# A retention and mixture-of-experts kernel on one core: the first chunk in four transfers with its values on GpSimd and six filling products, one expert choice behind the masks, one eviction ahead of three transposes, and the last block scaled by ScalarE alone

## The chip, the cores and the metric

The kernel runs on one core of a Trainium2 chip. The metric is the device time of one execution in microseconds (us); several executions are timed and their median is taken. In the profile, PE is TensorE (matrix products), PEld its loading of stationary operands, DVE is VectorE, ACT is ScalarE, POOL is GpSimd and SP is SyncE, which here issues nearly all loads. A letter q behind an engine's name (SPq) marks its instruction queue, where transfers are issued.

## The reference, cut to what matters

```python
# q, k, v: (4, 8, 768, 64) float32, that is batches, heads, tokens, width of a head
state = zeros(B, H, D, D)
for t in range(S):
    state = gamma[h] * state + outer(k[:, :, t], v[:, :, t])
    y[:, :, t] = scale * (q[:, :, t] @ state)
x = y.transpose(0, 2, 1, 3).reshape(3072, 512)

logits = x @ w_gate                            # 8 experts
expert_idx = argmax(logits, axis=1)
gate_w = softmax(logits)[expert_idx]
for e in range(8):
    xe = x[expert_idx == e]
    out[expert_idx == e] = gate_w * (relu(xe @ w1[e]) @ w2[e])   # 512 -> 1024 -> 512
```

## The kernel before

**Two stages.** The first is the retention (until some 105 us of the profile's clock), the second the experts (until 392 us). The 3072 tokens are cut into 24 chunks `g` of 128 tokens, six to a batch (`CPB`); `c = g % CPB` is the place in the batch. The retention is computed chunk by chunk in closed form: scores of a chunk against itself under a causal mask, plus the carried state.

**A chunk's steps.** `load(g)` brings the chunk's 1 MB in four parts of 512 columns: q turned, k turned, v natural, k natural (256 KB each). `scale(g)` multiplies v by the decay constants (`vs`), on GpSimd or VectorE. `scores(g)` makes 8 products of q and k into two PSUM tiles `sp` (one for each of the two heads of a pair), and VectorE multiplies each by the mask into `Sb`. `update(g)` adds the chunk to the state `U`, and ScalarE copies it to `ub`. `carry(g)` multiplies q by the state of the chunk before, into `Y`; `output(g)` adds the scores times the values to `Y`, and VectorE evicts `Y`, scaled, into `xT`. `rows(g)` turns `xT` back to token rows (`tr`, copied by ScalarE to `xrow`), and `logits` makes the gate's logits of two chunks (`lp`, `lg`).

**Gating.** The chunks' tokens are gated in six groups (`GROUPS`, first chunk and count). For each group, "choose" finds the largest logit on VectorE (`mx`, `ed`, `EA`, the one-hot choice), "soft" prepares the softmax with ScalarE, "rank" counts the tokens of each expert ahead of each token with the product `pf` on PE (`EA` against a triangle `us`), "slots" makes of it a row number (`KEY`), "weights" the softmax weight (`GW`), "label" writes both into the row. Then GpSimd scatters the rows, sorted by expert, to memory (`x_sorted`). Group 2 holds chunks 12 to 15; its choice stands at the end of chunk 16.

**Experts.** Each expert's tokens are fetched sorted, turned by VectorE (`turn_slices`, STREAM_TRANSPOSE), and split in a high part (ScalarE) and a low part (VectorE or GpSimd), as the weights are; each product of float32 precision is three products of high and low parts (`ph` into the hidden layer, `py` out of it). Before the retention has ended, the first 320 rows of expert 0 are fetched and turned (`turn_early`, in chunk 22), and pieces of their products (`fill`) stand between the last gating steps. `py` blocks of 128 rows are scaled by the gate weight into `yo` (`put_rows`), and GpSimd scatters them to the output. The last block of the last expert has 104 rows.

**What sets the order.** The program is under `tc.manual_schedule()`: each engine works off its instructions in the order in which the code is written, and semaphores order the engines against each other. SP's transfers take eight counters in turn, so its ninth waits for the first to have landed. Chunks 0 to 3 are loaded in halves of two parts each; the first is issued ahead of everything else. The constants `cs` and the small operand `gs` of the decay table are issued by ScalarE's queue. While PE has no data, it runs `WARM = 10` filling products into `warm` (128x512, bf16), and later one product makes the decay table (`decay`, copied to `buf`, where `G` lies). The score buffers `sp` are two, so the scores of the next chunk wait for the masks of this one.

## Time and profile before

| | |
|---|---|
| runs, median (lowest to highest) | 399.66 us (399.08 to 399.91), 3 runs |
| profiled execution: its time, its span | 400.06 us, 398.3 us |
| mean granted clock of PE in the profiled execution | 0.995 |
| PE busy | 390.3 us, 98% of the span, 3236 instructions |
| PEld busy | 356.5 us, 89% |
| DVE busy | 240.3 us, 60% |
| POOL busy | 185.2 us, 46% |
| ACT busy | 142.4 us, 36% |
| bytes moved | 81.53 MB, mean 205 GB/s |

The span is the time between the first and the last instruction of the profile; the execution's own time holds 1.76 us more. The rows by line that are shown below begin with the start and the busy time of a group (in us), then engine, line, operation, output and inputs with their tile shapes, and the number of instructions; in square brackets stands how long the engine was idle just before, and what ended that. The line numbers are those of the kernel before.

### The profile page before, as it was taken

To read this page: it belongs to the slowest core of one execution; us is meant where nothing else is said; L and a number is where in the kernel's file an instruction comes from. 1 tells how busy PE (TensorE), PEld (TensorE's weight loads), DVE (VectorE), ACT (ScalarE), POOL (GpSimd) and SP (SyncE) were. 2 spreads that over 40 slices of the span, in tenths; PEclk is the share of its full clock that TensorE was granted. 3 is DMA by queue.
4 is the path that set the end of the run, shared out by engine and by line. 5 is a ranking of instruction groups with operands and counts; after the bars stand their busy time and mean duration, and the time that the engine had idled before them with its cause. 6 is when DMAs were issued, how large, how long until landed. Compare 5 with 4: busy or idle time off the path is not lost. (4 is left out here: it accounts for less than half of the span.)

```text
span 398.3 us, 8240 instructions
## 1 busy us (share of the span) xinstructions
PE 390.3 (98%) x3236; PEld 356.5 (89%) x3236; DVE 240.3 (60%) x468; ACT 142.4 (36%) x249; POOL 185.2 (46%) x176
## 2 busy tenths in 40 slices
PE   8999999999999999999999999999999999999994
PEld 4888878787899889999999999999999999999972
DVE  3555757685744578573866477477737657665310
ACT  2224435224411455531542344054334416423100
POOL 1647959655260517200584077028406813740741
PEclk9999999999999999999999999999999999999998
DMA  8999999975058839547452755465564647430111
GB/s 273 422 419 420 418 416 420 324 297 149 2 216 174 327 117 305 214 167 162 166 182 92 190 183 213 84 209 165 177 152 157 234 83 232 146 133 0 54 47 48
DMA packets 42316, 81.53 MB, mean 205 GB/s; under 512 B 4444, under 2 KB 18144, under 8 KB 39844
## 3 DMA queue, kind: packets, MB, share of 16 engines
q1 hardware_dynamic: 36768, 67.46, 51.2%
q0 software_dynamic: 5360, 13.49, 9.1%
q8 instruction: 26, 0.43, 0.4%
q14 instruction: 14, 0.11, 0.1%
q10 hardware_dynamic: 148, 0.04, 0.1%
HBM read 65.90 MB, written 15.68 MB: 205 GB/s over the span
## 5 line engine op out<-in xcount | busy, mean ns | idle before, releaser
L738 POOL DMA_INDIRECT out<-Z,sidx x90 | 104.9, 1165 | 138.8 <-DVE Z L894 113.5
L133 DVE TENSOR_TENSOR wlo<-raw,whi 128x1024 fp32r<-128x1024 f32 x54 | 65.5, 1215 | 14.1 <-ACT whi L132 13.8
L132 ACT CAST whi<-raw 128x1024 fp32r<-128x1024 f32 (+1 forms) x72 | 67.3, 950 | 7.3 <-DMA raw<-w 7.3
L1034 PE MATMUL py<-hl,whi 128*128 128x452 f32 (+5 forms) x192 | 67.0, 349 | 0.0
L1034 PE MATMUL py<-hh,wlo 128*128 128x452 f32 (+5 forms) x192 | 66.8, 348 | 0.0
L1034 PE MATMUL py<-hh,whi 128*128 128x452 f32 (+5 forms) x192 | 66.8, 348 | 0.0
L1014 ACT ACTIVATE hh<-ph 128x452 fp32r<-128x452 f32 (+6 forms) x56 | 28.3, 507 | 81.5 <-PE ph L1009 81.5
L1009 PE MATMUL ph<-xh,wlo 128*128 128x452 f32 (+6 forms) x224 | 50.1, 345 | 0.0
L1009 PE MATMUL ph<-xh,whi 128*128 128x452 f32 (+6 forms) x224 | 50.1, 345 | 0.0
L1009 PE MATMUL ph<-xl,whi 128*128 128x452 f32 (+6 forms) x224 | 50.0, 345 | 0.0
L1015 DVE SCALAR_TENSOR_TENSOR hl<-ph,hh 128x452 fp32r<-128x452 f32 (+6 forms) x56 | 32.0, 574 | 29.7 <-ACT hh L1014 29.2
L1009 PEld LDWEIGHTS ph<-xh,whi 128*128 128x128 f32 x224 | 40.8, 188 | 0.8
L1009 PEld LDWEIGHTS ph<-xh,wlo 128*128 128x128 f32 x224 | 40.8, 188 | 0.8
L1009 PEld LDWEIGHTS ph<-xl,whi 128*128 128x128 f32 x224 | 40.7, 188 | 0.7
L1034 PEld LDWEIGHTS py<-hh,wlo 128*128 128x128 f32 x192 | 36.0, 188 | 0.8
L1034 PEld LDWEIGHTS py<-hl,whi 128*128 128x128 f32 x192 | 36.0, 188 | 0.7
L1034 PEld LDWEIGHTS py<-hh,whi 128*128 128x128 f32 x192 | 36.0, 188 | 0.7
L251 DVE TENSOR_TENSOR Sb<-sp,cs 128x512 f32<-128x512 f32 x48 | 30.8, 684 | 7.4 <-PE sp L248 7.4
L760 ACT CAST xh<-buf 128x512 fp32r<-128x512 f32 (+7 forms) x26 | 14.3, 556 | 56.5 <-DVE buf L753 56.5
L133 POOL TENSOR_TENSOR wlo<-raw,whi 128x512 fp32r<-128x512 f32 (+1 forms) x18 | 24.9, 1403 | 12.7 <-ACT whi L132 10.5
L738 POOL DMA_INDIRECT x_sorted<-xrow,KEY x24 | 24.2, 1010 | 13.1 <-issue 6.5
L889 DVE STREAM_TRANSPOSE Z<-py 128x416 f32<-128x416 f32 (+3 forms) x24 | 15.0, 626 | 24.4 <-PE py L1034 24.4
(163 smaller groups left out, 535.3 us busy)
## 6 DMA issues: line engine op xcount, KB each, us to landing
raw<-w SPq DMA_DIRECT2D x32, 1024.0 KB, 5.6
qkv_w<-qkv SPq DMA_DIRECT2D x12, 1024.0 KB, 18.3
qkv_t<-qkv SPq DMA_DIRECT2D x7, 1024.0 KB, 17.8
qkv_t<-qkv SPq DMA_DIRECT2D x8, 512.0 KB, 6.8
buf<-x_sorted SPq DMA_DIRECT2D x12, 211.2 KB, 4.8
x_sorted<-cs SPq DMA_DIRECT2D x6, 260.0 KB, 5.6
buf<-x_sorted SPq DMA_DIRECT2D x8, 195.0 KB, 4.7
out<-Z,sidx POOLq DMA_INDIRECT x90
```

The costliest lines, as they stand in the source:

```text
L132: nc.scalar.copy(out=hi[:, h], in_=raw[:, h])
L133: engine.tensor_tensor(out=lo[:, h], in0=raw[:, h], in1=hi[:, h].bitcast(F32), op=ALU.subtract)
L251: nc.vector.tensor_tensor(out=Sb[:, r], in0=sps[r], in1=causal.unsqueeze(1).broadcast_to([P, NP, C]), op=ALU.mult)
L738: sc = tc.nc.gpsimd.indirect_dma_start(out=dst, out_offset=bass.IndirectOffsetOnAxis(ap=index, axis=0), in_=rows, in_offset=None, bounds_c ...
L760: nc.scalar.copy(out=xh[:, :, c0:c0 + w], in_=xt[:, :, t0:t0 + w])
L889: nc.vector.transpose(out=Zs[e][:, 0:nb, k, :], in_=py[:, 0:32 * nb].rearrange("p (j c) -> p j c", c=32))
L1009: nc.tensor.matmul(out=ph[:, :cap], lhsT=wparts[e, f // 4][a][:, kd, fo:fo + P], rhs=x[:, kd, :cap], start=(n == 0), stop=(n == 3 * KD - 1))
L1014: nc.scalar.activation(out=hh[:, :cap], in_=ph[:, :cap], func=AF.Relu)
L1015: nc.vector.scalar_tensor_tensor(out=hl[:, :cap], in0=ph[:, :cap], scalar=0.0, in1=hh[:, :cap].bitcast(F32), op0=ALU.max, op1=ALU.subtract)
L1034: nc.tensor.matmul(out=py[:, :cap], lhsT=a[:, f % 4, k * P:(k + 1) * P], rhs=x[:, :cap], **se)
```

## The change

Five places are edited.

1. **The start.** Chunk 0 comes in four transfers of 256 KB and chunk 1 in a half and two quarters. The host lays q and k out anew, so that the first quarter holds q and k of the head pairs 0 and 1, and the second those of the pairs 2 and 3; `turned(g, i, r, p)` finds them. ScalarE's queue issues the constants `cs` ahead of `gs`. The values of chunk 0 are scaled by GpSimd. Six filling products instead of ten.
2. **Chunk 1.** The carry products stand ahead of the update.
3. **The third choice.** "choose" and "soft" of group 2 stand in chunk 17 (`FULL - 1`), behind the masks of chunk 18, instead of at the end of chunk 16, and its weights behind its slots.
4. **The early turns.** All three pieces of `turn_early` stand behind `output(22)`; before, the first stood ahead of it.
5. **The last block.** One ScalarE instruction of 512 columns scales it; before, VectorE scaled the first half and ScalarE the second.

```diff
-WARM = 10
+WARM = 6
...
-        def turned(g, i):
-            return qs[g][:, i].rearrange("a (p t) -> a p t", p=NP)
+        def turned(g, i, r, p):
+            at = i * 2 * C + p % 2 * C
+            return qs[g][half[r], p // 2, at:at + C]
...
-        def turn_early(i):
+        def turn_early():
...
-            part = pieces[1:] if i else pieces[:1]
-            for j, w, _ in part:
+            for j, w, _ in pieces:
                 turn_slices(nc, xt0, first["xg"], j, w)
...
-        load(0, halves[0])
+        quarters = [slice(i, i + 1) for i in range(4)]
+        load(0, quarters[0])
         gs = buf[0:2, 4 * NP * C:4 * NP * C + P + NP * C]
+        nc.scalar.dma_start(out=cs[:, 0:NFIRST], in_=cst[:, 0:NFIRST])
         nc.scalar.dma_start(out=gs, in_=gdec)
-        nc.scalar.dma_start(out=cs[:, 0:NFIRST], in_=cst[:, 0:NFIRST])
-        load(0, halves[1])
-        for part in halves:
+        for part in quarters[1:]:
+            load(0, part)
+        for part in (halves[0], *quarters[2:]):
             load(1, part)
...
-        scale(0, nc.vector)
+        scale(0)
...
+        def choose_group(i):
+            stages[i] = gating(i)
+            stages[i]["choose"]()
+            stages[i]["soft"]()
...
             if 1 < g < last:
                 scores(g + 1)
-            if g in ranked:
+            if g == FULL - 1:
+                choose_group(2)
+            elif g in ranked:
                 stages[ranked[g]]["weights"]()
...
-            if g == 1:
-                update(g)
             if g < last:
                 carry(g)
             if g == 1:
+                update(g)
                 scores(g + 1)
...
-            if g == last - 1:
-                turn_early(0)
             output(g)
...
             if g == last - 1:
-                turn_early(1)
+                turn_early()
...
                 if g != FULL + 1:
                     s["slots"]()
+                if g == FULL - 1:
+                    s["weights"]()
                 s["advance"]()
...
-        parts = (slice(0, 2), slice(2, 4)) if e == E1 and j == len(widths[e]) - 1 else (slice(0, 4),)
-        for i, k in enumerate(parts):
-            args = dict(out=sliced(yo[:w, :])[:, k], in_=featured(py[:w, :])[:, k])
-            if i:
-                nc.scalar.activation(func=AF.Copy, scale=meta[:w, j, 1:2], **args)
-            else:
-                nc.vector.tensor_scalar(in0=args["in_"], out=args["out"], scalar1=meta[:w, j, 1:2], scalar2=None,
-                                        op0=ALU.mult)
+        args = dict(out=sliced(yo[:w, :]), in_=featured(py[:w, :]))
+        if e == E1 and j == len(widths[e]) - 1:
+            nc.scalar.activation(func=AF.Copy, scale=meta[:w, j, 1:2], **args)
+        else:
+            nc.vector.tensor_scalar(in0=args["in_"], out=args["out"], scalar1=meta[:w, j, 1:2], scalar2=None, op0=ALU.mult)
```

PE at the start of the program, before: the last filling product, the scores of chunk 0 (one wait for the first half's counter), the decay table, the update (it waits for `vs` from DVE), and the output products.

```order
L489 MATMUL warm<-ones 128x512
L248 MATMUL sp<-qkv_t 128x128 [waits DMAHW1_49]
L248 MATMUL sp<-qkv_t 128x128 x7
L510 MATMUL decay<-buf 128x512 [waits DMAHW0_49]
L263 MATMUL U<-vs,qkv_t 64x64 [waits DMAHW3_49,DVE_49]
L263 MATMUL U<-vs,qkv_t 64x64 x7
L287 MATMUL Y<-Sb,vs 64x128 [waits DVE_49]
```

The same place on PE, of the changed kernel:

```order
L487 MATMUL warm<-ones 128x512
L249 MATMUL sp<-qkv_t 128x128 [waits DMAHW1_49]
L249 MATMUL sp<-qkv_t 128x128 x3
L249 MATMUL sp<-qkv_t 128x128 [waits DMAHW3_49]
L249 MATMUL sp<-qkv_t 128x128 x3
L508 MATMUL decay<-buf 128x512 [waits DMAHW2_49]
L264 MATMUL U<-vs,qkv_t 64x64 [waits DMAHW5_49,Pool_49]
L264 MATMUL U<-vs,qkv_t 64x64 x7
L287 MATMUL Y<-Sb,vs 64x128 [waits DVE_49]
```

The score products now wait for two counters, one for each quarter, and the update waits for the values from GpSimd (Pool) instead of VectorE.

DVE in chunks 16 and 17, before: `lg` closes the logits, the rows from `mx` to `sh` are the third choice, the two rows `Sb` are the masks of chunk 18, `GW` the weights, and `rk` takes up the ranking product `pf`.

```order
L348 TENSOR_REDUCE lg_1168<-lp 128x16 [waits PE_49]
L371 TENSOR_REDUCE mx_1243<-lg_1168 128x4 [waits DVE_49]
L372 TENSOR_REDUCE lp<-lg_1168 128x32 [waits Activation_49]
L373 TENSOR_TENSOR lp<-lp,mx_1243 128x32 [waits DVE_49]
L374 TENSOR_TENSOR lp<-lp,cs 128x32 [waits DVE_49]
L377 TENSOR_REDUCE ed_1244<-lp 128x4 [waits DVE_49]
L378 TENSOR_TENSOR EA<-lp,ed_1244 128x32 [waits DVE_49]
L380 TENSOR_TENSOR sh_1251<-lp,mx_1243 128x32
L251 TENSOR_TENSOR Sb<-sp,cs 128x512 [waits PE_49] x2
L413 TENSOR_REDUCE GW<-exs 128x4 [waits Activation_49]
```

The same place on DVE, of the changed kernel:

```order
L348 TENSOR_REDUCE lg_1167<-lp 128x16 [waits PE_49]
L252 TENSOR_TENSOR Sb<-sp,cs 128x512 [waits DVE_49,PE_49]
L252 TENSOR_TENSOR Sb<-sp,cs 128x512 [waits PE_49]
L371 TENSOR_REDUCE mx_1257<-lg_1167 128x4 [waits DVE_49]
L372 TENSOR_REDUCE lp<-lg_1167 128x32 [waits Activation_49]
L373 TENSOR_TENSOR lp<-lp,mx_1257 128x32 [waits DVE_49]
L374 TENSOR_TENSOR lp<-lp,cs 128x32 [waits DVE_49]
L377 TENSOR_REDUCE ed_1258<-lp 128x4 [waits DVE_49]
L378 TENSOR_TENSOR EA<-lp,ed_1258 128x32 [waits DVE_49]
L380 TENSOR_TENSOR sh_1265<-lp,mx_1257 128x32
```

The masks have moved ahead of the seven instructions of the choice; the weights (`GW`) now stand further down, behind `KEY`.

DVE in chunk 22, before: `xt` are the three transposes of the early rows (the first waits for their fetch), `xT` is the eviction of the chunk's output.

```order
L348 TENSOR_REDUCE lg_1625<-lp 128x16 [waits PE_49]
L753 STREAM_TRANSPOSE xt_1649<-xg_1542 128x4x4x32 [waits DMAHW6_49,DMAHW5_49,DMAHW7_49,DMAHW0_49,Pool_49]
L293 TENSOR_TENSOR xT<-Y,buf 128x4x128 [waits PE_49]
L753 STREAM_TRANSPOSE xt_1649<-xg_1542 128x4x4x32
L753 STREAM_TRANSPOSE xt_1649<-xg_1542 128x2x4x32
```

The same place on DVE, of the changed kernel:

```order
L348 TENSOR_REDUCE lg_1624<-lp 128x16 [waits PE_49]
L293 TENSOR_TENSOR xT<-Y,buf 128x4x128 [waits PE_49,Pool_49]
L757 STREAM_TRANSPOSE xt_1658<-xg_1541 128x4x4x32 [waits DMAHW2_49,DMAHW1_49,DMAHW3_49,DMAHW0_49,Pool_49]
L757 STREAM_TRANSPOSE xt_1658<-xg_1541 128x4x4x32
L757 STREAM_TRANSPOSE xt_1658<-xg_1541 128x2x4x32
```

The eviction has changed places with the first transpose.

More of the change, by code (lines that the diff above doesn't have):

```diff
@@ L243, in scores @@
             Sb = wk.tile([P, 2, NP, C], F32, name="Sb")
-            q, kt = turned(g, 0), turned(g, 1)
             sps = [ps_s.tile([P, NP, C], F32, name="sp") for _ in range(2)]
@@ L247, in scores @@
                 for r in range(2):
-                    nc.tensor.matmul(out=sps[r][:, p, :], lhsT=kt[half[r], p, :], rhs=q[half[r], p, :],
+                    nc.tensor.matmul(out=sps[r][:, p, :], lhsT=turned(g, 1, r, p), rhs=turned(g, 0, r, p),
                                      start=True, stop=True)
@@ L271, in carry @@
             if c > 0:
-                q = turned(g, 0)
                 for m in range(2):
@@ L277, in carry @@
                             nc.tensor.matmul(out=Y[half[o], r, m * C:(m + 1) * C], lhsT=ubs[(g - 1) % 3][half[r], p, :],
-                                             rhs=q[half[r], p, :], start=(m == 0), stop=False, skip_group_check=True)
+                                             rhs=turned(g, 0, r, p), start=(m == 0), stop=False, skip_group_check=True)
         def output(g):
@@ L437, in fetch_early @@
             fetch_rows(xg0, 0, NJ0)
-        def turn_early(i):
+        def turn_early():
             pieces = [(a // 32, min(P, EARLY - a), eng)
                       for a, eng in zip(range(0, EARLY, P), (nc.gpsimd, nc.vector, nc.vector))]
-            if i == 0:
-                first["xt"] = rawp.tile([P, KD, EARLY], F32, name="xt0", tag="raw")
-                first["x"] = [wp.tile([P, KD, EARLY], F32R, name=n, tag="w", bufs=11) for n in ("xh0", "xl0")]
-                early.extend(early_pieces(tc, wk, wp, ps_m, ps_s, ps_1, wparts, first["x"], first))
-            xt0, x = first["xt"], first["x"]
-            part = pieces[1:] if i else pieces[:1]
-            for j, w, _ in part:
+            xt0 = rawp.tile([P, KD, EARLY], F32, name="xt0", tag="raw")
+            first["x"] = x = [wp.tile([P, KD, EARLY], F32R, name=n, tag="w", bufs=11) for n in ("xh0", "xl0")]
+            early.extend(early_pieces(tc, wk, wp, ps_m, ps_s, ps_1, wparts, x, first))
+            for j, w, _ in pieces:
                 turn_slices(nc, xt0, first["xg"], j, w)
-            for j, w, _ in part:
+            for j, w, _ in pieces:
                 cut_high(nc, x[0], xt0, j, w)
-            for j, w, eng in part:
+            for j, w, eng in pieces:
                 cut_low(nc, eng, *x, xt0, j, w)
@@ L593, in retention_moe @@
                 nc.scalar.copy(out=wgs[:, :, 0:E], in_=k_("gates").rearrange("p (k e) -> p k e", k=NP))
-            if g in chosen or g == last:
-                i = chosen.get(g, 4)
-                s = stages[i] = gating(i)
-                s["choose"]()
-                s["soft"]()
+            if g in chosen and g != FULL - 2:
+                choose_group(chosen[g])
+            if g == last:
+                choose_group(4)
             if g == last:
@@ L1161 @@
     arrays = {
-        "qkv": np.stack([transposed(q), transposed(k), natural(v), natural(k)], axis=3).reshape(NCH, P, 4, DM),
+        "qkv": np.concatenate([np.stack([transposed(a).reshape(NCH, P, 2, 2 * C) for a in (q, k)], axis=3)
+                               .reshape(NCH, P, 2, DM), natural(v).reshape(NCH, P, 1, DM),
+                               natural(k).reshape(NCH, P, 1, DM)], axis=2),
         "w1": reordered(moe_w1, 1), "w2": np.ascontiguousarray(moe_w2), "cst": cst, "gdec": gdec,
```

## The prediction

> **What bounds the kernel now.** I read the page first, then the cores, then the order in time at each place that the change touches.
>
> ```profile
> span 398.3 us, 8240 instructions
> core 0: 398.3 us, clock 0.995
> ```
>
> PE carries the program nearly from end to end, so the question at each place is which wait of PE the edit shortens, and whether PE then meets another one. The mean clock says how long PE ran at half rate: 0.005 of 398.3 us is 1.99 us lost, that is 3.98 us at half. The first product starts at 1.08 (below), so full rate came at about 5.06.
>
> The start, in order of time (start, duration, engine, line, operation; in brackets what ended the idle time before it):
>
> ```profile
> 1.08 4.35 PE L489 MATMUL warm<-ones 128*128 128x512 bf16 x10 [1.08 <-DVE ones L155]
> 5.36 1.16 PE L248 MATMUL sp<-qkv_t 64*128 64x128 f32 x16
> 6.45 1.12 PE L510 MATMUL decay<-buf 2*128 2x512 f32 x2
> 6.64 0.69 DVE L235 TENSOR_TENSOR vs<-qkv_t,cs 128x512 f32<-128x512 f32 x1 [4.94 <-DMA cs<-cst]
> 7.25 1.28 DVE L251 TENSOR_TENSOR Sb<-sp,cs 128x512 f32<-128x512 f32 x2
> 7.50 0.69 PE L263 MATMUL U<-vs,qkv_t 128*64 128x64 f32 x16
> 7.61 0.59 ACT L511 COPY buf<-decay 128x512 f32<-128x512 f32 x1 [4.40 <-PE decay L510]
> 8.23 0.37 ACT L266 COPY ub<-U 128x256 f32<-128x256 f32 x1
> 8.59 0.88 PE L287 MATMUL Y<-Sb,vs 128*64 128x128 f32 x12 [0.16 <-DVE Sb L251]
> 9.08 1.04 POOL L235 TENSOR_TENSOR vs<-qkv_t,cs 128x512 f32<-128x512 f32 x1 [7.98 <-DMA qkv_t<-qkv]
> 9.39 1.16 PE L248 MATMUL sp<-qkv_t 64*128 64x128 f32 x16
> 10.58 1.29 DVE L251 TENSOR_TENSOR Sb<-sp,cs 128x512 f32<-128x512 f32 x2 [0.31 <-PE sp L248]
> 11.70 1.39 PE L248 MATMUL sp<-qkv_t 64*128 64x128 f32 x16
> 13.48 0.38 SPq L124 DMA_DIRECT2D raw<-w  x1
> 14.63 1.16 PE L248 MATMUL sp<-qkv_t 64*128 64x128 f32 x16
> ```
>
> PE runs ten filling products until 5.36, one every 0.43 us, and chunk 0's score products follow at once. U then waits for the scaled values (vs), which DVE makes only at 6.64, because the constants cs come late. DVE does the masks (Sb) after that, so the output products pause until 8.59.
>
> When a transfer lands is read from SP. Each transfer takes one of eight counters in turn, and SP's ninth waits until the first has landed, so the row that takes up a counter again marks a landing:
>
> ```profile
> 4.82 0.34 SPq L222 DMA_DIRECT2D qkv_t<-qkv  x1
> 10.97 0.33 SPq L222 DMA_DIRECT2D qkv_w<-qkv  x1
> ```
>
> The first is chunk 0's first half (512 KB); the second is chunk 2's first half. The row at 13.48 above marks chunk 3's first half in the same way. The rates of the transfers, stretch by stretch (last column GB/s; the fourth row is a stretch of weight loads with rows of 2 KB, as the quarters have):
>
> ```profile
> 2.00:3.00 1.00, 1.00 (x4) 0.36 (x3) 0.00 (x0) 1.00 (x1) 0.00 (x0) 1.00 0.79 217
> 3.00:4.00 1.00, 1.00 (x3) 0.30 (x2) 0.00 (x0) 0.19 (x1) 0.00 (x0) 1.00 0.95 250
> 10.00:20.00 10.00, 10.00 (x170) 8.06 (x168) 5.87 (x10) 2.41 (x6) 6.66 (x8) 1.00 1.03 422
> 172.00:173.70 1.70, 1.70 (x10) 1.56 (x9) 1.16 (x2) 0.81 (x1) 0.00 (x0) 1.00 1.05 411
> ```
>
> **The start: quarters, constants first, vs on GpSimd, six products.** Six products end at 1.08 + 6 x 0.43 = 3.64. The first quarter is half of what landed at 4.82. At 217 to 250 GB/s, 256 KB less take 1.0 to 1.2 us less, so it lands at 3.6 to 3.8. It may land as late as 4.8, where the half landed (the last rival), and not much before 3.0, since 217 GB/s move only 217 KB in the row from 2.00 to 3.00; I take 3.7. PE answers about 0.15 later, at 3.85. Half of the score products (0.42 at full rate, so 0.85 at half) end at 4.7. The second quarter lands like the old half, at 4.8, and the other half runs from 4.95 to 5.4. The decay product follows and takes 1.05 (6.45 to 7.50), to 6.45. The values are the third quarter: 256 KB at 422 are 0.62 us, so 5.4 to 5.5. The constants start ahead of the second quarter and should be in by then. GpSimd pays 1.04 (row 9.08) where DVE paid 0.69, so vs stands at 6.65, and U starts 0.17 later (7.33 to 7.50 before) at 6.8, against 7.50. That the gate for U moves to POOL delays nothing there: POOL's next work, the values of chunk 1, came in at 9.08 and comes about 0.6 earlier as a quarter. The fourth quarter lands at 6.1 to 6.4, before U needs it.
>
> DVE is free for the masks at 5.6 and done by 6.9, so the pause ahead of 8.59 goes. U and the output products are 0.51 + 0.98, which brings chunk 1's scores to 8.3 instead of 9.39. They, the carry product and U of chunk 1 (the swap of these two costs nothing: both stand between the same neighbours, 9.39 + 1.09 to 11.70) take 2.31 us and end at 10.6.
>
> There PE meets the next wait: chunk 2 lands at 10.97. Its bytes are the same, and SP's three more issues are hidden, because the transfers already queued last past 8 us. But 1.5 MB now come in rows of 2 KB, at 411 instead of 422 at worst, 0.1 us more. So chunk 2's scores start at 11.1 to 11.25 against 11.70. They took 1.39 there and 1.16 elsewhere, because the masks of chunk 1 freed the score buffers late (10.58 + 1.29); these masks are early now, and 0.23 goes too. Gain 0.45 to 0.6 and 0.23: I take **0.75**. Chunk 3 landed at 13.48 for products at 14.63, so it allows 1.0, and from there nothing on PE waits for a load. A bound from above is 1.09 (what chunk 1's scores gain), from below 0 while the clock opens as before.
>
> **The third choice behind the masks (g = 17).**
>
> ```profile
> 75.48 1.16 PE L248 MATMUL sp<-qkv_t 64*128 64x128 f32 x16
> 76.09 0.19 DVE L371 TENSOR_REDUCE mx<-lg 128x4 f32<-128x32 f32 x1
> 77.10 0.19 DVE L378 TENSOR_TENSOR EA<-lp,ed 128x32 bf16<-128x32 f32 x1
> 77.17 0.43 PE L287 MATMUL Y<-Sb,vs 128*64 128x128 f32 x2
> 77.30 1.28 DVE L251 TENSOR_TENSOR Sb<-sp,cs 128x512 f32<-128x512 f32 x2
> 78.18 1.03 PE L287 MATMUL Y<-Sb,vs 128*64 128x128 f32 x14 [0.57 <-issue]
> 79.14 0.19 PE L387 MATMUL pf<-EA,us 128*128 128x32 bf16 x1
> ```
>
> The choice (mx to EA, 1.20 us) moves from the gap in which DVE waits for the scores to behind the masks. Masks start 1.19 after their scores (9.39 to 10.58), so at 76.67, and end at 77.9; EA then ends at 79.1, and the ranking products (pf) can start at 79.15. They start at 79.14 now, because PE lost about 0.8 us between 77.17 and 78.18, waiting for nothing that the profile shows. So PE has to wait for EA exactly as long as that pause lasted: **0**, whether the pause comes again or not, within 0.1. The masks that come 0.6 earlier help nobody, since the scores that need their buffers stand behind pf. On DVE the values and the eviction behind the choice are 0.6 later, and the weights move behind the keys, with ACT's label behind them: 1.2 us on ACT, which PE meets again only at its logits, and it is idle enough there. At worst 0.3.
>
> **The eviction ahead of the early turns (g = 22).**
>
> ```profile
> 98.94 1.05 PE L287 MATMUL Y<-Sb,vs 128*64 128x128 f32 x16
> 99.59 0.71 DVE L753 STREAM_TRANSPOSE xt<-xg 128x512 f32<-128x512 f32 x1 [1.61 <-DMA xg<-x_sorted]
> 100.23 0.65 DVE L293 TENSOR_TENSOR xT<-Y,buf 128x512 f32<-128x512 f32 x1
> 101.03 0.67 PE L277 MATMUL Y<-qkv_t,ub 64*64 64x128 f32 x16 [0.23 <-ACT xh L760]
> 101.53 0.93 ACT L760 CAST xh<-xt 128x512 fp32r<-128x512 f32 x2 [0.57 <-DVE xt L753]
> 103.06 0.54 PE L793 MATMUL ph<-xh,whi 128*128 128x320 f32 x2
> ```
>
> PE waits for xT (100.88 + 0.15). Y ends at 99.95, so without the transpose xT runs from 100.05 to 100.7 and PE starts at 100.87: **0.16** gained. The three transposes then follow from 100.6, the last cast of xh ends at about 102.8 (102.46 before), and the early products want it at 102.9. That cover is 0.1 thin; past it the gain shrinks to 0. Between 0 and 0.25.
>
> **The last block by ScalarE alone.**
>
> ```profile
> 391.99 0.39 PE L1032 MATMUL py<-whi,hl 128*104 128x512 f32 x1
> 392.42 0.48 DVE L881 TENSOR_SCALAR yo<-py,meta 104x256 f32<-104x256 f32 x1 [4.81 <-PE py L1032]
> 392.94 0.47 ACT L879 ACTIVATE yo<-py,meta 104x256 f32<-104x256 f32 x1 [16.74 <-DVE yo L881]
> 393.72 1.01 POOL L738 DMA_INDIRECT out<-yo,sidx  x1 [4.86 <-ACTq L725]
> ```
>
> The two halves run one after the other: ACT waited for DVE. One ACT instruction of 512 columns costs 0.47 and the 256 columns more, priced by 0.59 - 0.37 = 0.22 (rows 7.61 and 8.23): 0.69, from 392.42 to 393.11 instead of 393.41. All behind it follows: **0.30**. Between 0.2 (as if the longer row cost half as much again) and 0.4.
>
> **Sum.** 0.75 + 0 + 0.16 + 0.30 = 1.2 us. The profiled execution took 400.06 (the span and 1.76 around it), 0.40 above the median of 399.66. Its sum is 398.85; against the median the same gain gives 398.5. A measurement tells 0.2%, 0.8 us, from no change.
>
> **Rivals.**
> A later clock: PE has a gap at 3.64 and a broken stream until 5. If that starts the count again, full rate comes 3.98 after 3.85, at 7.8. The scores then end at 5.7, decay at 7.6, U at 8.25, output at 9.25, and chunk 2's scores start at 11.55 and end 0.35 earlier instead of 0.75: 398.9. Against it: the gap is 0.2 us in 4, and at 77.17 PE paused 0.8 without leaving full rate (the mean clock has no room for it). [...]
>
> The pause at 77.17 is an accident of the profiled run (its time lies above all three others). Where the usual run has no pause, PE would be 0.75 earlier there (masks end at 78.58, the next scores start then instead of at 79.35), and the moved choice takes just that away: 399.2.
>
> Slower: the clock opens two stretches late, at 3.85 + 2 x 3.98 = 11.8, if products that fill half the rows and wait for quarters do not count as work. PE is then at half rate for all of chunks 0 and 1; every microsecond past 7.8 costs 0.5, and chunk 2's scores end 1.6 later than before: 400.8. It decides from an opening at about 9.5 on.
>
> The quarters land no earlier than the half: then the scores run from 4.95 to 6.0, U starts at 7.1, and chunk 2's landing still decides. The time stays.
>
> **Chances.** As forecast 0.52 (its own range 398.0 to 398.8), a later clock 0.20, no pause in the usual run 0.20, slower 0.08. Of the forecast about 0.44 lie beyond 0.2%, of the two middle ones together another 0.10: faster 0.54, same 0.37, slower 0.09. The range goes from 397.6 (the upper bounds 1.09 + 0.25 + 0.4 give 397.9, less 0.3 for a median of three runs, since the three shown lie 0.8 apart) to 399.8, which leaves out the slow case.
>
> **What the next profile would show.** The first scores at about 3.85 in two pieces; U near 6.8, released by POOL; no pause in the first output products; chunk 2's scores at 11.1 to 11.25, released by the DMA; pf released by DVE's EA about 1.0 behind the output products; the carry of chunk 23 about 1.95 behind the output of chunk 22; one ACT row of 104x512 near 0.69 and the scatter 0.3 behind it; a mean clock of 0.995. A clock of 0.990 or less, or scores of twice their length after 5.1, make it wrong.

## The result, and the profile after

The changed kernel takes 401.61 us in the median of 15 runs (400.41 to 403.56), against 399.66 (15 runs, 399.01 to 400.43) before: a ratio of 1.0054, with a 95% interval of 1.0035 to 1.0074. It is slower, where 1.2 us of gain were forecast. Its runs fall apart: seven lie at 400.41 to 400.81, two at 401.61 and 402.36, six at 403.10 to 403.56. Even the lowest is above the median of before. The profiled execution took 403.19, 3.13 above that of before (400.06), so it belongs to the upper group.

The head of its page and the row of its core:

```profile
span 401.4 us, 8237 instructions
core 0: 401.4 us, clock 0.996
```

The start on PE, GpSimd and VectorE, in the timeline (columns as before):

```profile
1.08 2.74 PE L487 MATMUL warm<-ones 128*128 128x512 bf16 x6 [1.08 <-DVE ones L155]
4.17 2.28 PE L249 MATMUL sp<-qkv_t 64*128 64x128 f32 x16 [0.34 <-DMA qkv_t<-qkv]
5.97 1.04 POOL L237 TENSOR_TENSOR vs<-qkv_t,cs 128x512 f32<-128x512 f32 x1 [4.88 <-DMA qkv_t<-qkv]
6.37 2.07 PE L508 MATMUL decay<-buf 2*128 2x512 f32 x2
8.37 1.12 PE L264 MATMUL U<-vs,qkv_t 128*64 128x64 f32 x16
9.28 1.92 PE L287 MATMUL Y<-Sb,vs 128*64 128x128 f32 x16
11.13 1.90 PE L249 MATMUL sp<-qkv_t 64*128 64x128 f32 x16
12.96 0.67 PE L277 MATMUL Y<-qkv_t,ub 64*64 64x128 f32 x16
14.18 1.39 PE L249 MATMUL sp<-qkv_t 64*128 64x128 f32 x16
```

The data come 0.3 to 0.4 later than forecast (first scores at 4.17 against 3.85, values done at 7.01 against 6.65). But every product up to 12.9 takes nearly twice as long as in the profile of before: the decay product 2.07 instead of 1.12, the output products 1.92 instead of 1.09 without a wait, chunk 1's scores 1.90 instead of 1.16. Full rate opens at 12.7. (The trace keeps a record of the granted clock, from which the profile's clock figures are averaged. Its first entry, full rate, is at 12.72 us. The profile counts the time ahead of the first entry as 1.00, though the products there take twice their time.) Chunk 2's scores start at 14.18 instead of 11.70: **2.48 lost**.

Chunk 17:

```profile
79.06 0.67 PE L277 MATMUL Y<-qkv_t,ub 64*64 64x128 f32 x16
79.66 1.09 PE L287 MATMUL Y<-Sb,vs 128*64 128x128 f32 x16
81.37 0.19 DVE L378 TENSOR_TENSOR EA<-lp,ed 128x32 bf16<-128x32 f32 x1
81.71 0.19 PE L387 MATMUL pf<-EA,us 128*128 128x32 bf16 x1 [0.96 <-DVE sh L380]
```

PE now waits 0.96 for the choice, where it paused before. From the carry to the ranking products there are 2.65 us against 2.57: 0.09 lost.

Chunks 22 and 23, first of before, then of the changed kernel:

```profile
101.03 1.28 POOL L767 TENSOR_TENSOR xl<-xt,xh 128x512 fp32r<-128x512 f32 x1 [2.90 <-ACT xh L760]
102.18 1.03 DVE L767 TENSOR_TENSOR xl<-xt,xh 128x512 fp32r<-128x512 f32 x2 [0.36 <-ACT xh L760]
103.26 0.68 DVE L293 TENSOR_TENSOR xT<-Y,buf 128x512 f32<-128x512 f32 x1
104.86 0.19 DVE L378 TENSOR_TENSOR EA<-lp,ed 128x32 bf16<-128x32 f32 x1
105.79 0.19 PE L387 MATMUL pf<-EA,us 128*128 128x32 bf16 x1
109.93 0.75 PE L793 MATMUL ph<-xh,whi 128*128 128x320 f32 x4
```

```profile
103.28 1.62 DVE L757 STREAM_TRANSPOSE xt<-xg 128x512 f32<-128x512 f32 x3
103.52 0.67 PE L277 MATMUL Y<-qkv_t,ub 64*64 64x128 f32 x16
104.72 1.27 POOL L771 TENSOR_TENSOR xl<-xt,xh 128x512 fp32r<-128x512 f32 x1 [4.01 <-ACT xh L764]
105.26 1.61 DVE L771 TENSOR_TENSOR xl<-xt,xh 128x512 fp32r<-128x512 f32 x2 [0.36 <-ACT xh L764]
106.93 0.68 DVE L293 TENSOR_TENSOR xT<-Y,buf 128x512 f32<-128x512 f32 x1
108.53 0.19 DVE L378 TENSOR_TENSOR EA<-lp,ed 128x32 bf16<-128x32 f32 x1
108.87 0.18 PE L387 MATMUL pf<-EA,us 128*128 128x32 bf16 x1
111.93 0.19 PEld L816 LDWEIGHTS acc<-hh,whi 128*128 128x128 f32 x1 [0.36 <-ACT xrow L305]
113.35 0.75 PE L797 MATMUL ph<-xh,whi 128*128 128x320 f32 x4
```

The carry of chunk 23 starts at 103.52 against 101.03, so the edit gained 0.08 there (2.57 late before it, 2.49 after). Then VectorE falls behind: its two low parts take 1.61 instead of 1.03, the eviction of chunk 23 comes 3.67 later than before, the choice EA 3.67, the ranking products 3.08, and the second batch of early products 3.42. PE has **lost 0.93** between 103.5 and 113.4. In the profile of before, GpSimd's low part was nearly done (102.31) when VectorE began its own; now the two run side by side.

The end:

```profile
395.41 0.39 PE L1032 MATMUL py<-whi,hl 128*104 128x512 f32 x1
395.84 0.69 ACT L880 ACTIVATE yo<-py,meta 104x512 f32<-104x512 f32 x1 [16.22 <-PE py L1032]
396.83 1.01 POOL L742 DMA_INDIRECT out<-yo,sidx  x1 [4.55 <-ACTq L729]
```

The last product is 3.42 later, the scatter 3.11: 0.31 gained. The sum is 2.48 + 0.09 - 0.08 + 0.93 - 0.31 = 3.11, and the measured difference of the two profiled executions 3.13: the rows account for it. This is the sum for one execution of the upper group, not for the median.

### The profile page after: what moved, and what is told of

Its sections match the earlier page's. It is cut to its first block, busy times and chain, and to the rows that moved or that the text cites. A ratio compares the mean times of both kernels' runs of the same rounds, so it can differ in the third digit from the quotient of the medians.

```text
span 401.4 us, 8237 instructions
## 1 busy us (share of the span) xinstructions
PE 393.0 (98%) x3232; PEld 358.8 (89%) x3232; DVE 240.7 (60%) x466; ACT 141.9 (35%) x249; POOL 185.8 (46%) x177
## 4 chain that ended last, share of the span: by engine, by line
issue 39%; PE 35%; POOL 16%; DMA 5%; DVE 2%; ACT 1%; POOLq 1%; DVEq 0%; ACTq 0%
POOL out L742 16%; PE sp L249 7%; PE Y L287 5%; DMA out<-Z,sidx 4%; PE acc L816 3%; PE U L264 3%; PE Y L277 3%; PE ph L797 3%; PE tr L304 3%; PE ph L1009 2%; PE L L332 2%; PE py L928 1%; PE hn L911 1%; PE lp L344 1%; DMA qkv_t<-qkv 1%
## 5 line engine op out<-in xcount | busy, mean ns | idle before, releaser
L293 DVE TENSOR_TENSOR xT<-Y,buf 128x512 f32<-128x512 f32 x24 | 16.6, 690 | 26.0 <-PE Y L287 23.9
```

The costliest lines, as they stand in the source:

```text
L293: nc.vector.tensor_tensor(out=xT.rearrange("a (r m) t -> a r m t", m=2), op=ALU.mult, in0=Y[:, :, 0:2 * C].rearrange("a r (m t) -> a r m t ...
```

## The experiments

The kernels are either the changed one with something undone, or the one before with one edit. Medians are against the kernel before in the same comparison (399.65, 399.60, 407.76 and 399.74; the third is on a chip where everything took 2% longer, and only its differences are used). The ratio and its interval weigh all runs and are not the quotient of the two medians; where a kernel's runs fall into groups the two differ.

### Ten filling products again

```diff
-WARM = 6
+WARM = 10
```

> The changed kernel with ten filling products instead of six; all else as changed. Theory 1 (the shorter fill opens a gap, and PE stays at half rate until about 12.6 us in many runs): full rate opens near 5, as in the kernel before, the scores of chunk 2 start at about 11.3, the runs no longer reach 402 to 403.6 and lie in one group at about 399.9, which is the median of before, +0.94 for the early turns, +0.09 for the choice, -0.08 for the eviction, -0.33 for the tail, and -0.45 for the start. Rival (the quarters, the host layout or the order of the constants slow the start by themselves): the runs still reach 402 to 403.6, and the first products of chunk 1 still take twice their length.

400.89 (400.27 to 401.32, 12 runs), ratio 1.0023 (1.0010 to 1.0036). One group, none above 401.4: the upper group hangs on the fill. But it is 1.0 above the 399.9 expected. Full rate opens at 5.16 in this profile and at 5.19 in that of before, so the two can be set side by side. Its start on PE:

```profile
5.34 1.16 PE L249 MATMUL sp<-qkv_t 64*128 64x128 f32 x16
7.48 0.69 PE L264 MATMUL U<-vs,qkv_t 128*64 128x64 f32 x16
8.00 1.05 PE L287 MATMUL Y<-Sb,vs 128*64 128x128 f32 x16
8.97 1.16 PE L249 MATMUL sp<-qkv_t 64*128 64x128 f32 x16
10.71 0.69 PE L264 MATMUL U<-vs,qkv_t 128*64 128x64 f32 x16
12.23 1.16 PE L249 MATMUL sp<-qkv_t 64*128 64x128 f32 x16 [0.84 <-DMA qkv_t<-qkv]
```

The pause in the output products is gone, as forecast, and chunk 1's scores come at 8.97 instead of 9.39 (the prediction had 8.3, with six products). Then PE waits 0.84 for chunk 2's transfer, until 12.23, where the prediction had 11.1 to 11.25. The start has lost 0.45 by 22.6 instead of gaining. With that, 0.45 + 0.09 - 0.09 + 0.93 - 0.31 = 1.07; its profiled execution took 401.12, 1.06 above that of before.

### The old early turns

```diff
-            output(g)
+            if g == last - 1:
+                turn_early(0)
+            output(g)
...
-                turn_early()
+                turn_early(1)
```

> The changed kernel with the early turns in two parts as before (first transpose ahead of the eviction of chunk 22). Theory 2 (VectorE and GpSimd form their low parts at the same time, VectorE's two take 1.61 instead of 1.03, and the late eviction of chunk 23 and the late choice behind it cost PE 0.94): all runs are 0.86 shorter, the lower ones at about 399.7 and the higher ones, still at half rate until 12.6, at about 402.5; the low parts on VectorE take 1.03 again. Rival (the loss behind 101 us is a consequence of the later start, since transfers and scatters keep their own times): no gain, 400.6 and 403.3.

401.24 (399.39 to 402.82, 12 runs), ratio 1.0034 (1.0014 to 1.0054): the lowest runs 1.0 below those of the changed kernel, the highest 0.7. In the profile nothing is lost between chunk 23 and the early products. Theory 2 holds. Its profiled execution (401.35) shows a second thing. Its rows by stretch (the last three columns are the granted clock, the share of the transfers and GB/s), then PE's rows:

```profile
1.00:4.00 3.00, 2.74 (x6) 0.74 (x6) 0.70 (x8) 1.47 (x2) 0.10 (x1) 1.00 0.56 153
4.40:7.80 3.40, 2.37 (x20) 1.37 (x22) 1.29 (x2) 0.58 (x1) 1.04 (x1) 1.00 1.01 313
7.90:11.10 3.20, 3.20 (x38) 2.87 (x38) 0.53 (x1) 0.37 (x1) 1.65 (x2) 0.50 1.03 384
11.30:14.00 2.70, 2.70 (x57) 2.34 (x56) 1.29 (x2) 0.37 (x1) 1.58 (x3) 1.00 1.02 411
```

```profile
4.28 1.36 PE L249 MATMUL sp<-qkv_t 64*128 64x128 f32 x16 [0.46 <-DMA qkv_t<-qkv]
7.72 1.02 PE L264 MATMUL U<-vs,qkv_t 128*64 128x64 f32 x16 [1.03 <-POOL vs L237]
8.54 1.92 PE L287 MATMUL Y<-Sb,vs 128*64 128x128 f32 x16
```

By the clock record, full rate opens at 4.46 (the scores take 1.36, not 2.28), falls back at 7.88 (the granted clock reads 0.50) and opens again at 11.29: the three points lie 3.42 and 3.41 us apart. In the stretch from 4.4 to 7.8 PE was busy for 2.37 us, half of it with the two-row decay product. One such fall-back lowers the mean clock by 0.004 (half of 3.41 us in 399.5). Four of the twelve runs here have a mean of 0.992 or 0.993, and the changed kernel's two middle runs 0.991. That these runs fell back too is read from their means alone: only this one was profiled.

### Six filling products in the kernel before

```diff
-WARM = 10
+WARM = 6
```

> The kernel before with six filling products instead of ten; all else as before. PE then has a gap from 3.8 until chunk 0's first half at about 5.0. Theory 1: full rate opens late, in most runs at 8 to 12.6, and the time rises by 0.7 to 2.7: 400.4 to 402.4 in the median. Rival (the late opening comes from the quarters: products that wait for each transfer at half rate): full rate opens by about 8 and the time rises by at most 0.3, to 399.9.

402.62 (399.03 to 403.11, 12 runs), ratio 1.0053 (1.0030 to 1.0075): the short fill alone costs as much as the whole change, and the median lies above the 402.4 that was the upper end expected. In the profile full rate opens at 13.8; until then the scores take 2.08, chunk 1's too, though they wait for nothing:

```profile
4.84 2.08 PE L248 MATMUL sp<-qkv_t 64*128 64x128 f32 x16 [1.02 <-DMA qkv_t<-qkv]
11.61 2.08 PE L248 MATMUL sp<-qkv_t 64*128 64x128 f32 x16
```

This kernel has no quarters, so these are not needed for a late opening. Chunk 17 of this execution stands in the old order and shows no pause:

```profile
79.71 0.67 PE L277 MATMUL Y<-qkv_t,ub 64*64 64x128 f32 x16
80.31 1.09 PE L287 MATMUL Y<-Sb,vs 128*64 128x128 f32 x16
81.33 0.19 PE L387 MATMUL pf<-EA,us 128*128 128x32 bf16 x1
```

From the carry to the ranking products there are 1.62 us, not 2.57.

### Ten filling products and the old turns

The changed kernel with two of these edits together: ten filling products, and the early turns in two parts.

> The changed kernel with ten filling products and with the early turns in two parts as before. If theories 1 and 2 both hold, what is left of the change is the start (-0.45), the choice (+0.09) and the tail (-0.33): 399.0, 0.7 below the kernel before. If the start brings nothing with the fill of ten, 399.4. If both theories are wrong, above 400.5.

400.17 (399.42 to 400.43, 12 runs), ratio 1.0008 (0.9995 to 1.0021). This is 0.7 below ten products alone, on the same chip, so the turns' loss is confirmed. But it lies 0.8 above even the 399.4 expected if the start brought nothing: chunk 2's scores start at 12.26, 0.56 later than in the profile of before, so the start loses with ten products too.

### Halves instead of quarters

```diff
-        load(0, quarters[0])
+        load(0, halves[0])
...
-        for part in quarters[1:]:
-            load(0, part)
-        for part in (halves[0], *quarters[2:]):
+        load(0, halves[1])
+        for part in halves:
             load(1, part)
```

(on top of the last one)

> The changed kernel with ten filling products, the early turns in two parts, and chunks 0 and 1 loaded in halves (512 KB, 4 KB rows) as before; order of the constants, values on GpSimd, carry ahead of update, choice and tail as changed. Theory 3 (rows of 2 KB move slower at the start, so chunk 2's scores, which waited 0.84 for their transfer with quarters and started at 12.23, can start earlier): chunk 2's scores start at 11.1 to 11.3, and the time falls by 1.0 from 400.17 to about 399.2. Rival (the transfers are late because the constants go first or because of the fill): chunk 2's scores start at 12 again and the time stays at 400.1.

399.59 (399.35 to 400.08, 12 runs), ratio 0.9998 (0.9990 to 1.0007): by the medians 0.58 less than with quarters, but on another chip, and the two intervals overlap. In its profiled execution full rate opened only at 6.9, so PE came to chunk 2's scores at 12.06, and found their data there. The rows of the stretch from 4 to 9, of before, of the changed kernel with ten filling products, and of this one:

```profile
4.00:9.00 5.00, 4.84 (x50) 2.67 (x50) 1.89 (x3) 0.96 (x2) 0.00 (x0) 1.00 1.05 388
```

```profile
4.00:9.00 5.00, 5.00 (x56) 2.91 (x54) 1.29 (x2) 0.96 (x2) 1.04 (x1) 1.00 1.01 342
```

```profile
4.00:9.00 5.00, 5.00 (x42) 2.97 (x42) 1.29 (x2) 0.59 (x2) 1.15 (x2) 1.00 1.04 406
```

388 and 406 GB/s with halves, 342 with quarters: 0.2 to 0.3 MB less in this stretch, which is 0.6 to 0.8 us of transfer. The other traces agree: 303 to 342 in all eight profiles with quarters, 383 to 406 in all ten with halves. Whether the shorter rows or the greater number of transfers do it was not separated. The order of the constants, the rival, is not excluded for the landing itself: with the constants first, SP takes up the counter of chunk 2's first half at 10.54 here, but at 11.67 in the next experiment, which has halves as well. The time fell by 0.6, not by the 1.0 expected: PE got there later in this execution, and the run times don't show the rest.

### Start and tail alone, in the kernel before

```diff
-        nc.scalar.dma_start(out=gs, in_=gdec)
         nc.scalar.dma_start(out=cs[:, 0:NFIRST], in_=cst[:, 0:NFIRST])
+        nc.scalar.dma_start(out=gs, in_=gdec)
...
-        scale(0, nc.vector)
+        scale(0)
```

(and the last block by ScalarE alone)

> The kernel before with three edits alone: the constants ahead of the decay operand on ScalarE's queue, the values of chunk 0 on GpSimd, and the last block by one ScalarE instruction. Ten filling products, halves, the old place of the choice, the old early turns. Expected: chunk 1's scores at 8.97 instead of 9.39 (as with the fill of ten), chunk 2's at 11.1 to 11.3 instead of 11.70, the scatter of the last block 0.33 earlier: 0.8 in all, 398.9. If the transfers of the halves also land later: 399.3 to 399.6. In the profile PE either pauses in chunk 17 for 0.8 with nothing that releases it, or it does not; without the pause 0.7 less.

399.52 (398.56 to 400.26, 12 runs), ratio 0.9994 (0.9983 to 1.0004): a miss of the 398.9. It lies in the 399.3 to 399.6 named for the case that the transfers of the halves land later too, and in the profile they do. With the constants first, chunk 0's first half comes later (PE waits 0.39 for it, until 5.48), U starts at 7.92, and chunk 2's scores at 11.79, right behind their landing (11.67, against 10.97 before). The masks' gain is given back there.

### The decay product over 128 rows

```diff
-        gs = buf[0:2, 4 * NP * C:4 * NP * C + P + NP * C]
+        gs = buf[:, 4 * NP * C:4 * NP * C + P + NP * C]
+        nc.vector.memset(gs, 0.0)
...
-        nc.scalar.dma_start(out=gs, in_=gdec)
+        nc.scalar.dma_start(out=gs[0:2], in_=gdec)
```

(and the clearing of `wgs`, which stood first on VectorE, further down)

> The changed kernel with its decay product over 128 rows instead of 2 (the other 126 rows are zero; same result, same number of products), six filling products. Theory 1b (a stretch of 3.4 us in which PE mostly runs the two-row product counts as idle, so that full rate waits for the next stretch or falls back): the opening comes at 9.3 at the latest, nothing falls back, and no run is above 402; median about 400.7. Rival (what counts is the gap behind the fill, or the score products with half the rows): two groups again, about 400.5 and 403.3.

401.65 (400.43 to 403.21, 6 runs), ratio 1.0053 (1.0034 to 1.0071), a miss: 400.7 was expected and no run above 402, and two are. So a late opening does not need the two-row product (only an early one, at 3.75, was profiled). But no run has a mean clock under 0.997.

### The choice alone, in the kernel before

```diff
+            if g == FULL - 1:
+                stages[2] = gating(2)
+                stages[2]["choose"]()
+                stages[2]["soft"]()
-            if g in ranked:
+            elif g in ranked:
                 stages[ranked[g]]["weights"]()
...
-            if g in chosen or g == last:
+            if (g in chosen and g != FULL - 2) or g == last:
...
+                if g == FULL - 1:
+                    s["weights"]()
```

> The kernel before with the third choice behind the masks, and nothing else. PE waits 0.96 for the choice in every execution. Theory 4 (the pause of 0.8 that PE makes in chunk 17 of the kernel before comes in some executions only, and without it the old order is 0.7 to 0.95 ahead): 0.1 slower in executions with the pause, 0.7 to 0.9 without: median 400.0 to 400.4. Rival (the pause comes in every execution of the old order): 399.75.

400.13 (399.84 to 400.36, 11 runs), ratio 1.0009 (1.0000 to 1.0017). The lowest run lies 0.75 above the lowest of before (399.09): the short executions are gone. In every profile with the new place the ranking products start 2.65 to 2.66 after the carry. With the old place it was 2.57 to 2.60 three times (with the pause) and 1.62 to 1.63 twice (without); on the slower chip it was 1.62 to 1.63 in all three such profiles, but there PE paused in chunk 16 instead (two gaps of 0.36 to 0.43 at 76 to 78, released by nothing the profile shows). With the new place the pause costs nothing where it comes, since PE would wait for the choice anyway: this profile has it (0.60), that of the changed kernel has not, and both come to 2.65 or 2.66.

### The turns alone, and without GpSimd

The kernel before with all three early transposes behind the eviction; in the second kernel VectorE also makes all low parts:

```diff
-                      for a, eng in zip(range(0, EARLY, P), (nc.gpsimd, nc.vector, nc.vector))]
+                      for a, eng in zip(range(0, EARLY, P), (nc.vector, nc.vector, nc.vector))]
```

> The kernel before with the eviction of chunk 22 ahead of all three early transposes, and nothing else. Theory 2: PE gains 0.08 at the carry of chunk 23 and loses 0.94 up to 110 us, since the low parts on VectorE take 1.7 beside GpSimd's instead of 1.1, and the eviction of chunk 23 and the choice of group 4 come 1.2 later: 0.86 slower, 400.5. Rival (what was lost there came from the later start of the whole program): 399.5.

> As the last one, with the first low part on VectorE too, so that GpSimd does nothing there. Theory 2a (the two engines stand in each other's way: 1.27 for 128x512 beside GpSimd, 0.69 alone): three rows of 0.69, 0.69 and 0.42 on VectorE, 1.8 in all against 1.69, the eviction of chunk 23 as late as before or 0.1 later, and the time about 400.5 to 400.6. Rival (the long row of 1.27 is VectorE's own, from the order of its instructions): a row of 1.2 or more again, 2.4 in all, and 401.0 or more.

409.02 (408.06 to 409.64, 6 runs), ratio 1.0031 (1.0019 to 1.0043), and 408.37 (407.97 to 409.02, 11 runs), ratio 1.0013 (1.0004 to 1.0022). The first loses 0.94 in its profile at the same place. In the second the loss is 0.47: better than expected. The low parts on VectorE in groups of one shape (the number behind the bar is busy time and mean ns of one), of the changed kernel, then of the second:

```profile
L771 DVE TENSOR_TENSOR xl<-xt,xh 128x512 fp32r<-128x512 f32 x1 | 1.3, 1275 | 0.4 <-ACT xh L764 0.4
```

```profile
L761 DVE TENSOR_TENSOR xl<-xt,xh 128x512 fp32r<-128x512 f32 x2 | 1.3, 666 | 0.0
```

One such part takes 1275 ns beside GpSimd's (the two overlap for 0.73 us) and 666 without it, so VectorE does two in the time of one. Why one slows the other was not shown. The other half of the loss was not taken apart: what is left of the edit is that VectorE turns all three pieces before it does anything else.

### Eight filling products, and the decay rows again

```diff
-WARM = 6
+WARM = 8
```

> The changed kernel with eight filling products instead of six: the fill ends at 4.5, when the first quarter has landed, so PE has no gap there. Theory 1c (the gap makes the difference): no run above 402, one group at 400.3 to 401.3 as with ten. Rival 1d (what counts is that the fill's dense products take up nearly a whole stretch of 3.4 us, wherever it lies; the score products at half rate don't do it): some runs, two to four in twelve, still above 402.

410.25 (409.11 to 411.55, 6 runs), ratio 1.0069 (1.0056 to 1.0081), 2.5 above before. The gap is closed (the scores follow the fill at 4.60 without a wait), and it is no better: theory 1c falls. Four of the six runs have a mean clock of 0.993 or 0.994, and one of the other two is the highest. So it was run again, on another chip, beside the same kernel with the decay product over 128 rows.

> The changed kernel with eight filling products once more, beside the next two kernels. In four of its six runs on the chip before the mean clock was 0.993 to 0.994. Theory 1b: those are executions in which full rate opened early and fell back for one stretch while PE ran the two-row decay product and waited for the update's values. Then the runs at 0.994 or less come again, 1.5 to 3.5 above the kernel before. Rival: the clock figures belonged to that chip, and none comes here.

> The same with the decay product over 128 rows (126 of them zero). Theory 1b: no run with a mean clock of 0.994 or less, and a median about 1.0 to 1.5 below the kernel with the two-row product. Rival (the wait for the values is what lets the clock fall, whatever the rows): as many such runs as with two rows, and the same median.

401.28 (400.55 to 401.91, 4 runs), ratio 1.0043 (1.0027 to 1.0058), and 400.97 (400.38 to 401.37, 6 runs), ratio 1.0034 (1.0023 to 1.0046). Two of the four with two rows have 0.991 and 0.992, and these are the two longest; with 128 rows the lowest is 0.997. With the six-product pair that makes 8 runs of 25 with the mean clock of a fall-back with the two-row product, and none of 12 with 128 rows, though PE waits for the values there too (0.65 in both profiles). The two other kernels with six products and two rows have 7 such runs of 24. The kernel before, with ten, has one of the 106 in these comparisons: 402.24 with a mean clock of 0.992, where its median was 399.65. The medians differ by 0.3 only, less than the 1.0 to 1.5 expected; with so few runs that says little. With 128 rows the kernel is 1.23 above before, as it is with ten products (1.24): so what is left there is more likely the turns, the transfers and the choice than the clock.

### The tail alone, and with the values on GpSimd

> The kernel before with the last block scaled by one ScalarE instruction, and nothing else. One row of 0.69 after the last product, the scatter 0.3 earlier, 399.3 in the median. Rival (the scatter or the end waits for something else): no change, 399.6.

407.49 (406.94 to 408.42, 11 runs), ratio 0.9997 (0.9987 to 1.0007). The profile has the row of 0.69; the gain of 0.3 that was expected is below what the runs resolve.

```diff
-        scale(0, nc.vector)
+        scale(0)
```

> The kernel before with the values of chunk 0 on GpSimd and the last block by one ScalarE instruction; constants in the old order, halves, ten filling products, old choice, old turns. The masks no longer stand behind the values, so the output products of chunk 0 lose their pause of 0.44; the values come 0.2 to 0.35 later, since GpSimd takes 1.04 where VectorE took 0.69. Chunk 2's scores start at about 11.5 and take 1.16 instead of 1.39: 0.3 to 0.4, and 0.3 at the tail. Time 0.6 to 0.7 below the kernel before. Rival (the later values cost what the masks give): 0.3 below.

399.26 (398.50 to 400.42, 12 runs), ratio 0.9988 (0.9979 to 0.9998): 0.5 below the kernel before, between the 0.6 to 0.7 expected and the rival's 0.3, and, by the medians, 2.3 below the changed one. It is the only kernel here whose interval lies below 1, though by a hair. The masks no longer stand behind the values, and the output products run through (8.88, 1.05). Its profiled execution opened late (the scores of chunk 0 took 1.93) and had no pause in chunk 17, so the start's share can't be read from it.

> The kernel before once more, for a second look at chunk 17. Theory 4: the pause of 0.8 ahead of the last output products there comes in some executions only. One look shows it or not: with the pause about 2.57 from the carry products to the ranking products, without it 1.6 to 1.7.

This profile has the pause: 2.60.

## Why the prediction was wrong, step by step

**The moment of full rate, which went wrong first.** The sum priced scores, decay, U and output products at full rate from 5.06 on, and took that moment from the mean clock of 0.995. That number came from elsewhere. The rows by stretch of the kernel before, at its end:

```profile
390.00:395.00 5.00, 2.38 (x11) 1.42 (x9) 0.48 (x1) 0.47 (x1) 1.01 (x1) 0.93 0.04 12
395.00:398.20 3.20, 0.00 (x0) 0.00 (x0) 0.00 (x0) 0.00 (x0) 0.00 (x0) 0.50 0.21 58
```

The missing 0.005 is lost after the last product: by the clock record the half rate begins at 394.31, 3.98 us before the span ends. At the start the granted clock reads 1.00 while the products take twice their time, in the changed kernel too:

```profile
9.28:11.10 1.82, 1.82 (x20) 1.52 (x18) 0.00 (x0) 0.37 (x1) 1.33 (x2) 1.00 1.04 401
```

So the sign that the prediction named, a clock of 0.990 or less, could not come from a late opening (0.996); the other one, products of twice their length after 5.1, did. That the same 3.98 us, counted from 1.08, came out near the opening of that execution (5.19) was chance.

**The shorter fill.** The gap of 0.2 in 4 us was dismissed, and late opening got chances of 0.20 and 0.08. The runs show that the fill decides: no run of ten products on the changed kernel is above 401.4, six of 15 with six products are above 403. The slower rival had the right place (11.8; it was 12.7), but its price fell short: it put chunk 2's scores 1.6 late, and they were 2.48. Of its condition, half-filled rows and waits for quarters, the quarters are not needed: the kernel before opens late with six products and halves. Whether the half-filled rows matter was not tested. Both rivals on the clock had one shift of the opening, and none an opening that is lost again, as in the profile with the old turns (4.46, 7.88, 11.29).

What the fill decides here is a draw. The clock record's stretch at full rate is 389.12 us long in the profile of before and 385.71 in that of the changed kernel, 114 and 113 times 3.413, and the two stretches at the start of the profile with the old turns are 3.42 (full rate) and 3.41 (half). As an estimate from these four, the clock changed at whole steps of 3.413 us; the openings of the first two, 5.19 and 12.72, lie 7.53 apart, which is 2.2 steps, so the steps do not lie alike in every execution. With ten products full rate opened at 4.0 to 7.1 in all eleven profiles, a spread of less than one step; with six at 3.75, 4.46, 12.7 and 13.8. Counting such steps back from the opening (an estimate too, since the record has no entry ahead of it), a step that held 2.67 us of filling products and nothing else ended in full rate (once, at 3.75), and steps with 2.60, 2.52 and 2.40 of them did not (in the traces that opened later, at 7.1, 13.8 and 6.9). Six products are 2.74 us with a gap behind them, so by this estimate a step must hold nearly all of them; ten run on into the scores with a gap of 0.4 at most, and the next step is filled too. That reading fits these traces; where the steps lie was read, not controlled.

**"Chunk 2 lands ... 0.1 us more."** Mis-sized. By SP's row, chunk 2's first half lands at 11.3 to 12.1 in the eight profiles with quarters, and at 10.6 to 11.0 in the eight with halves and the constants in the old order: 0.9 more on average. The 411 GB/s came from weight loads in mid-program; seven transfers and the constants at the start ran at 342 against 388. With the next point this turned the start from -0.75 to +0.45 in the one pair of profiles in which the clock opened at the same time (5.16 and 5.19).

**"Scaled values, masks, no pause."** Half right. The pause goes, which gives 0.42 at chunk 1's scores with ten products, but the bound was 1.09: U was to start at 6.8, and in the five profiles with quarters that opened by 5.3 and did not fall back it starts at 7.3 to 7.5, no earlier than before (7.50, and 7.10 to 7.13 in the two other profiles of before's start that opened by 4.2). In four of the five PE waits there for GpSimd's values or the last quarter. A slip in the sum changed nothing: half of the score products are 0.54 at full rate (1.09 for all, 5.36 to 6.45), not 0.42, but by the sum U waits for the values in either case.

**The choice, 0.** Right against an execution with the pause (0.09). The rival "no pause in the usual run" was half right: the pause came there in three of five profiles of the old order and in none of the three of the slower chip. The new place takes its 2.65 whether PE pauses or not, against 1.62 in the old one without the pause.

**The eviction, -0.16, "past it the gain shrinks to 0".** The gain was 0.08, and the lower bound was wrong. The step followed PE to the early products and stopped. It didn't ask what stood behind the three transposes on VectorE: the low parts, the eviction of chunk 23, the choice of group 4, and at its end the ranking products on PE. Nor did it see that the low parts would now run beside GpSimd's. That is +0.93.

**The tail, -0.30.** Right: one row of 0.69 (0.69 forecast), 0.31.

## What to carry to other kernels

When PE needs a start-up fill, let it run on into the real products without a gap. As an estimate from the steps of 3.413 us read here, two of them, 6.8 us from the first product, hold a whole one wherever it begins (the latest opening with ten, 7.1, lies 6.0 behind that product). Judge it by the spread of the runs; here, trimming the fill to the arrival of the data cost more than the data brought. When an instruction is moved ahead of others on its engine, follow everything behind it until another engine takes it up, and look at which engine now runs at the same time. Read a mean only after asking in which stretch it was made.

## What was not expected of the hardware

The granted clock in the rows reads 1.00 during the half rate at the start, and 0.50 once full rate has been lost (7.88 to 11.29), so only durations, and the first entry of the clock record, show the first. In one profile full rate was lost 3.42 us after it came (4.46 to 7.88), and by their mean clocks 8 of 25 runs with a two-row product and a wait in that stretch did the same, none of 12 with 128 rows. In the two profiles of late opening it came at 12.7 and 13.8, though PE had been busy nearly without a gap since 4.2 and 4.8 (4.83 of the 5.00 us from 4 to 9 in the changed kernel); which of its work brings full rate stays open. Eight products opened by 5.3 in all three profiles, and six of their ten runs with two rows have the mean clock of a fall-back, which may be why they are no better in the median than six. VectorE's low part of 128x512 took 1275 ns where GpSimd's overlapped it for 0.73 us, 693 where it overlapped for 0.13 (before), and 666 where GpSimd made none. PE's pause of 0.6 to 0.8 in chunk 17, with nothing in the profile that releases it, comes in some executions and not in others; its cause was not found.
